# Long convolution and soft MoE: the convolution's first transform stage with tokens stationary, its results in one on-chip buffer, and the filter's spectrum read from DRAM

## The chip, the cores and the metric

The kernel runs on one core of one Trainium2 chip, in 32-bit floating point. The metric is the device time of one execution in microseconds; lower is better. Before the change three runs took 925.19, 927.99 and 931.83 us, median 927.99.

The engines go by short names: PE is TensorE's matmul and PEld its weight load, DVE is VectorE, ACT is ScalarE, POOL is GpSimd, SP is SyncE, which issues most DMAs here. A matmul of 32-bit numbers stands in the records twice (two passes, each with its weight load), so counts of records are twice the counts of matmuls.

## The reference

```python
def _attn_ref(x, h):                 # x (8, 5696, 128), h (5696, 128)
    L = 2 * S
    Xf = np.fft.rfft(x, n=L, axis=1)
    Hf = np.fft.rfft(h, n=L, axis=0)
    return np.fft.irfft(Xf * Hf[None], n=L, axis=1)[:, :S, :]

def _moe_ref(x, phi, w1, w2):        # x (45568, 128), phi (128, 32), 8 experts of 4 slots
    logits = x @ phi
    d = softmax of logits over the tokens
    slot_input = d.T @ x
    slot_out[e] = np.maximum(slot_input[e] @ w1[e], 0) @ w2[e]
    c = softmax of logits over the slots
    return c @ slot_out
```

A causal convolution of each of 128 channels with its own filter, along 5696 tokens and for 8 sequences ("batches"), and then a soft mixture of experts over all tokens.

## The kernel before, in words

The transform of length 2 x 5696 is split as N1 = 90 by N2 = 64: token 64 m + n is row m (89 rows, on partitions) and column n (64). A sequence passes through three stages. The filter h is treated as sequence 0, the batches as 1 to 8, so stages A and B run nine times, stage C eight times.

**Stage A** (`load_x` L179, `fold` L196, `stage_a` L205) works in eight steps per sequence. A step loads 4 columns and their 4 mirror columns (`xc`, three buffers, two DMAs), folds them into a sum and a difference on POOL (L201, 128x512), and multiplies each by two of the three tables in `s1`, which are stationary (L212: 128x128 weights, 512 moving columns: 4 columns by 128 channels). ACT copies each PSUM bank to `fst` (L214), and SP writes it to the DRAM buffer `f` (L218, two DMAs per half step, 1 KB runs).

**Stage B** works on frequencies. `f` is read back frequency by frequency into `gt` (`load_g` L230, 512 KB, up to two units ahead). A unit is two pairs of frequencies, 12 units per sequence. `stage_b1` (L241) does 8 matmuls of 64x64 weights by 256 columns (L250) into the PSUM tile `bt`; DVE multiplies `bt` by the real and the imaginary part of the filter's spectrum (L270, `Hr`, `Hi`, both kept on chip), and the products are added and subtracted into `yf` (L279: one of the two on POOL while `share` holds, that is before stage C begins and after stage A has ended, else both on DVE). For sequence 0 the same code makes `Hr` and `Hi` (L274). `stage_b2` (L283) does 8 more matmuls (L294) into `bz`, ACT copies them to `zst` (L299) and SP writes them to the DRAM buffer `z` (L302). `bt` and `bz` have one buffer each.

**Stage C** takes 8 columns ("a pair" T, 32 in all): `zc` is read from `z` (`load_pair` L322, one buffer), `stage_c1` (L336) finishes the inverse transform with matmuls (L349), a fold on DVE (L354, L355) and four adds on POOL (L368); `stage_c2` transposes (L377, ACT L379), `stage_c3` multiplies by phi (L386, ACT L389), `column_max` (L393) keeps a running maximum on DVE, `stage_c4` and `softmax` make both softmaxes (L411, L444), `dispatch` (L455) adds into the slots' sums, `stage_c6` stores the token weights. One pair takes two steps.

**The order of the work is written out by hand** in the loop at L563, and each engine does its instructions in that order. Step t does stage A of chunk t, stage B nine steps behind (LAG_B), stage C from step 27 on (LAG_C). Within a step: first half of stage A, `dispatch`, slot 1 of stage B, `stage_c1`, `stage_c2`, `stage_c6`, slot 2, `load_pair`, `load_x`, `stage_c5`, second half of stage A, `stage_c3`, slot 3, `column_max`, `softmax`. Steps have one unit of B (slot 2) and two units (slots 1 and 3) in turn. `stage_b2` of a unit comes in the slot after its `stage_b1`. Stage A ends after step 71, stage B after step 80. Then come the last pairs, the experts (L739 to L794) and the output (L809 to L836).

The four PSUM banks that `bank()` hands out in turn serve stages A and C together.

## Time and profile before

| what | value |
|---|---|
| median of three runs | 927.99 us |
| the profiled execution | 923.88 us, its span 922.1 us |
| mean granted TensorE clock | 0.943 |
| PE, DVE, ACT, POOL busy | 818.0, 653.1, 481.7, 488.1 us |
| stage A on PE (L212) | 576 records, 275.9 us |
| folds on POOL (L201) | 144, 192.8 us, 1342 ns each |
| stage A's evictions on ACT (L214) | 288, 171.9 us, 597 ns each |
| first matmul of stage B (L250) | at 52.65 us |
| DMA: f<-fst, gt<-f, z<-zst | 288 x 180 KB, 99 x 512 KB, 88 x 512 KB |
| the DMA queue of SP | 270.85 MB, 91.4% of the 16 engines' span |

How to read the profile: times are microseconds from the span's start unless marked ns. A group of instructions is line, engine, operation, output<-inputs, shapes and count, then busy time and the mean ns of one, then the idle time of its engine before them with what ended it. PE's matmuls are pipelined and the ends of their records are modelled, so a PE that is busy need not be at its peak, and the spacing of starts says more than a duration. A DMA engine counts as busy while it has a packet. Idle time of an engine that nobody waits for costs nothing.

### The profile page before, as it was taken

What the parts mean: (1) busy time and instruction counts of PE and PEld (TensorE: products, weight loads), DVE (VectorE), ACT (ScalarE), POOL (GpSimd) and SP (SyncE); (2) the same over time, 40 slices, a digit from 0 to 9 for tenths busy, and PEclk for the clock granted to TensorE, in tenths of its full rate; (3) what the DMA queues carried; (4) which work ended last, traced back from release to release, by engine and by line L of the source; (5) the groups of instructions that cost most, each with busy time, mean ns of one, the idle gap of its engine ahead of it and who ended that gap; (6) DMA issues with size and microseconds to landing.
All of it is one profiled execution on the core that took longest, in us unless ns stands there. A gap on an engine that the chain in (4) does not pass through costs nothing.

```text
span 922.1 us, 19325 instructions
## 1 busy us (share of the span) xinstructions
PE 818.0 (89%) x7220; PEld 423.9 (46%) x7220; DVE 653.1 (71%) x887; ACT 481.7 (52%) x888; POOL 488.1 (53%) x426
## 2 busy tenths in 40 slices
PE   6968898899999999999999999999987777878893
PEld 2323344345444445544554454444444434345783
DVE  3047665478888878888888788988887775674552
ACT  4623454455556655555666666656553344475442
POOL 4648766546655565556565655655466552472000
PEclk9989999899999999999999999999999888798865
DMA  9989999999899999999999999999989887761798
GB/s 298 279 274 299 272 345 311 289 345 327 268 320 319 314 282 324 316 314 285 341 304 327 289 324 329 297 318 320 316 269 330 272 254 198 211 249 73 272 405 341
DMA packets 156552, 272.45 MB, mean 295 GB/s; under 512 B 11766, under 2 KB 114422, under 8 KB 153317
## 3 DMA queue, kind: packets, MB, share of 16 engines
q1 hardware_dynamic: 155883, 270.85, 91.4%
q8 instruction: 58, 0.95, 0.4%
q10 hardware_dynamic: 576, 0.36, 0.2%
q14 instruction: 35, 0.29, 0.1%
HBM read 142.86 MB, written 128.21 MB: 294 GB/s over the span
## 4 chain that ended last, share of the span: by engine, by line
PE 51%; DMA 31%; POOL 5%; DVE 5%; issue 3%; SPq 2%; ACT 2%; DVEq 0%; POOLq 0%; ACTq 0%
PE bank L212 17%; DMA zc<-z 11%; PE bank L349 9%; DMA gt<-f 8%; PE bt L250 7%; PE bz L294 6%; DMA out_dram<-o 4%; PE bank L377 4%; DVE p L270 2%; POOL y L368 2%; DMA f<-fst 2%; PE bank L462 2%; DMA z<-zst 2%; PE bank L438 2%; PE bank L386 2%
## 5 line engine op out<-in xcount | busy, mean ns | idle before, releaser
L212 PE MATMUL bank<-x,s 128*128 128x512 f32 x576 | 275.9, 614 | 12.3 <-POOL x L201 12.0
L201 POOL TENSOR_TENSOR x<-xc 128x512 f32<-128x512 f32 x144 | 192.8, 1342 | 154.7 <-PE bank L212 70.4
L214 ACT ACTIVATE fst<-bank 128x512 f32<-128x512 f32 x288 | 171.9, 597 | 95.5 <-PE bank L212 74.8
L299 ACT ACTIVATE zst<-bz 128x1024 f32<-128x1024 f32 x96 | 93.2, 971 | 205.4 <-PE bz L294 198.5
L270 DVE TENSOR_TENSOR p<-bt,Hr 128x1024 f32<-128x1024 f32 x96 | 112.9, 1176 | 108.0 <-PE bt L250 95.7
L212 PEld LDWEIGHTS bank<-x,s 128*128 128x128 f32 x576 | 102.4, 193 | 131.5 <-issue 93.4
L279 DVE TENSOR_TENSOR yf<-p 128x512 f32<-128x512 f32 (+1 forms) x163 | 146.4, 931 | 3.3
L250 PE MATMUL bt<-gt,wt 64*64 64x256 f32 x1620 | 116.4, 394 | 25.1 <-DMA gt<-f 22.0
L349 PE MATMUL bank<-zc,i 128*64 128x512 f32 x480 | 117.1, 610 | 7.0 <-DMA zc<-z 4.1
L294 PE MATMUL bz<-yf,vt 64*64 64x256 f32 x1440 | 104.9, 393 | 15.5 <-POOL yf L279 15.0
L270 DVE TENSOR_TENSOR p<-bt,Hi 128x1024 f32<-128x1024 f32 x96 | 112.3, 1170 | 0.0
L250 PEld LDWEIGHTS bt<-gt,wt 64*64 64x64 f32 x1620 | 55.0, 134 | 102.0 <-issue 31.6
L368 POOL TENSOR_TENSOR y<-y,op 128x512 f32<-128x512 f32 x64 | 77.5, 1211 | 7.8 <-DVE op L354 5.1
L294 PEld LDWEIGHTS bz<-yf,vt 64*64 64x64 f32 x1440 | 58.2, 137 | 44.2 <-POOL yf L279 21.0
L279 POOL TENSOR_TENSOR yf<-p 128x512 f32<-128x512 f32 (+1 forms) x29 | 45.9, 1583 | 53.9 <-DVE p L270 53.9
L368 POOL TENSOR_TENSOR y<-y,om 128x512 f32<-128x512 f32 x54 | 71.8, 1330 | 2.1
L270 DVE TENSOR_TENSOR p<-bt,turn 128x1024 f32<-128x1024 f32 (+1 forms) x24 | 27.2, 1174 | 57.8 <-PE bt L250 57.7
L349 PEld LDWEIGHTS bank<-zc,i 128*64 128x64 f32 x480 | 30.8, 138 | 68.3 <-issue 40.8
L377 PE MATMUL bank<-ident,y 109*128 109x109 f32 x512 | 60.0, 275 | 0.7 <-DVE y L368 0.7
L377 PEld LDWEIGHTS bank<-ident,y 109*128 109x128 f32 x512 | 53.5, 151 | 13.6 <-issue 11.9
L379 ACT ACTIVATE yt<-bank 128x360 f32<-128x360 f32 x128 | 50.9, 482 | 3.3 <-PE bank L377 3.3
L819 PE MATMUL op<-so,cT 32*128 32x128 f32 x704 | 46.0, 374 | 4.4 <-ACT o L828 3.6
(97 smaller groups left out, 851.5 us busy)
## 6 DMA issues: line engine op xcount, KB each, us to landing
f<-fst SPq DMA_DIRECT2D x288, 180.0 KB
gt<-f SPq DMA_DIRECT2D x99, 512.0 KB
z<-zst SPq DMA_DIRECT2D x88, 512.0 KB
zc<-z SPq DMA_DIRECT2D x30, 1024.0 KB
xc<-in_x_dram SPq DMA_DIRECT2D x64, 320.0 KB
out_dram<-o SPq DMA_DIRECT2D x16, 1024.0 KB
zc<-z SPq DMA_DIRECT2D x30, 416.0 KB
out_dram<-o SPq DMA_DIRECT2D x8, 768.0 KB
```

The source lines that it names most:

```text
L201: nc.gpsimd.tensor_tensor(out=y_[:, :, :], in0=t_[:, 0, :, :], in1=t_[:, 1, ::-1, :], op=AL.subtract if comp else AL.add)
L212: nc.tensor.matmul(p[:, :], s1[:, tab[G], :], src[:, :, :].rearrange("p n d -> p (n d)"), start=True, stop=True)
L214: nc.scalar.activation(st[:, :, G, :], p[:, :].rearrange("p (n d) -> p n d", d=D), AF.Copy)
L250: nc.tensor.matmul(bt[q * HP:(q + 1) * HP, a, o, :], wt[r, 2 * i + q, :], t_[r, 2 * o + q, :, :].rearrange("p c d -> p (c d)"), start=True ...
L270: nc.vector.tensor_tensor(out=p_[r, 0:k, :, :], in0=pv, in1=h_, op=AL.mult)
L279: eng.tensor_tensor(out=y_[r, 0:k, c, :], in0=pr[r, 0:k, c, :], in1=pi[r, 0:k, 1 - c, :], op=op_)
L294: nc.tensor.matmul(bz[a * HP:(a + 1) * HP, q, o, :], vt[r, i, a, :], y_[r, a * m + o, :, :].rearrange("p c d -> p (c d)"), start=True, sto ...
L299: nc.scalar.activation(st[:, 0:m, 0:n, :].rearrange("p o q x -> p q o x"), bz[:, 0:n, 0:m, :], AF.Copy)
L349: nc.tensor.matmul(p[h_ * HP:(h_ + 1) * HP, :], i1[0:kr, tab, :], t_[0:kr, h_, o, :, q, :], start=True, stop=True)
L368: eng.tensor_tensor(out=part_, in0=part(v, 0), in1=o_[:, :, :], op=sign)
L377: nc.tensor.transpose(p[:, i * TR:(i + 1) * TR], ys[T][0:TR, k * CH + i, 0:D], ident[0:TR, 0:TR])
L379: nc.scalar.activation(yt[:, k * CH:(k + 1) * CH, :, :], of_tokens(p), AF.Copy)
```

## The change

- **Stage A with the tokens stationary.** The folded tokens become the weights (32 columns at a time, one channel, all 128 partitions) and the tables the moving operand (90 columns; 96 in every fourth matmul). One matmul gives 32 tokens by 90 table columns; four of them (sum and difference, two halves of the table) go to the four 32-column tiles of PE and fill the 128 partitions of one bank, four channels to a bank. A step of stage A is now 16 channels with all tokens of the sequence, where it was 8 columns with all channels. So all of a sequence's folds come before its first matmul.
- **`xf`, one buffer for a whole sequence.** Folded tokens lie there in one of two layouts by the parity of the sequence; the fold of the next sequence's chunk writes the places that stage A's step has just read. The weights are read at a step of 512 bytes (even) or 16 bytes (odd sequences). The 16 difference folds of sequences 0 and 1 go to DVE.
- **`ft` in place of the DRAM buffer `f`.** An 8 by 8 array of blocks, read along one axis by stage B and written along it by stage A of the next sequence, axes exchanged from sequence to sequence. ACT writes it from PSUM (DVE half of it for sequence 0), reading PSUM at a step of 90.
- **Stage B's units.** Eight groups of six frequencies per sequence, one per step: unit 0 has two pairs, unit 1 one pair (the last group one pair and a single frequency): 16 units per sequence instead of 12, the same matmuls. Both units are done before the step's stage A; slot 3 is gone.
- **The filter's spectrum in DRAM.** `Hr` and `Hi` are no longer on chip; sequence 0 makes `ht`, which is stored (786 KB per step), and read back in each step of the other sequences, two buffers.
- **Order.** LAG_B 8, LAG_C 26, the last step 79. `load_x` has two buffers, six during sequence 0 (four of them in `zc`). The products are added in place in `pr`. The loads of w1 begin one step earlier. Step t: `dispatch`, slot 1, `stage_c1`, `stage_c2`, `stage_c6`, slot 2, `load_pair`, `stage_c5`, all of stage A, the fold of chunk t+8, `load_x` of chunk t+10, `stage_c3`, `column_max`, `softmax`.

```diff
-    s1 = apool.tile([P, 3, P], F32, name="s1", tag="s1", bufs=1)
+    s1 = apool.tile([P, 2, 2, 2 * NP + 6], F32, name="s1", tag="s1", bufs=1)
+    xf = apool.tile([P, 2, HALF * D], F32, name="xf", tag="xf", bufs=1)
+    ft = fconst.tile([P, NJ, NJ, 2 * KG, DG], F32, name="ft")
...
-    xf = [apool.tile([P, CH, D], F32, name=f"x{i}", tag=f"x{i}", bufs=1) for i in range(2)]
-    xcs = [apool.tile([P, 2, CH, D], F32, name=f"xc{i}", tag=f"xc{i}", bufs=1) for i in range(3)]
-    for t_ in xcs:
-        nc.vector.memset(t_[:, :, :, :], 0.0)
+    zring = [ypool.tile([P, 2, 2, CH, 2, D], F32, name="zc")]
+    xcs = [apool.tile([P, 2, CH, D], F32, name=f"xc{i}", tag=f"xc{i}", bufs=1) for i in range(2)]
+    first = xcs + [zring[0][:, h_, o, :, :, :].rearrange("p n c d -> p (n c d)").rearrange(
+        "p (s n d) -> p s n d", s=2, n=CH)
+                   for h_ in range(2) for o in range(2)]
+    for i, t_ in enumerate(first):
+        (nc.gpsimd if i % 2 else nc.vector).memset(t_[:, :, :, :], 0.0)
...
-        t_ = xcs[c % len(xcs)]
+        t_ = first[c % len(first)] if g == 0 else xcs[c % len(xcs)]
...
-    folded = {}
-
-    def fold(c, comp):
-        if c not in xs:
+    def block(t_, g, r, k):
+
+        return t_[r, k, :] if g % 2 == 0 else t_[r, :, k]
+
+    def across(t_, g, r, k):
+
+        return t_[r, :, k] if g % 2 == 0 else t_[r, k, :]
+
+    def token_views(comp):
+
+        v = xf[:, comp, :]
+        return (v.rearrange("p (m d) -> p m d", d=D),
+                v.rearrange("p (e m f) -> p e m f", m=HALF, f=CH))
+
+    def fold(c):
+        if c >= (B + 1) * NJ:
             return
-        t_ = xs.pop(c) if comp else xs[c]
-        y_ = xf[comp]
-        nc.gpsimd.tensor_tensor(out=y_[:, :, :], in0=t_[:, 0, :, :], in1=t_[:, 1, ::-1, :],
-                                op=AL.subtract if comp else AL.add)
-        folded[(c, comp)] = y_
-
-    def stage_a(c, comp):
         g, j = divmod(c, NJ)
-        src = folded.pop((c, comp))
-        tab = (0, 1) if comp == 0 else (1, 2)
-        st = apool.tile([P, CH, 2, D], F32, name="fst", tag="fst", bufs=5)
-        for G in range(2):
+        t_ = xs.pop(c)
+        for comp in range(2):
+            eng = nc.vector if comp and g < 2 else nc.gpsimd
+            even, odd = token_views(comp)
+            if g % 2 == 0:
+                to, ab = even[:, CH * j:CH * (j + 1), :], (t_[:, 0, :, :], t_[:, 1, ::-1, :])
+            else:
+                to = odd[:, :, CH * j:CH * (j + 1), :].rearrange("p e n f -> p n e f")
+                ab = [v.rearrange("p n (e f) -> p n e f", f=CH)
+                      for v in (t_[:, 0, :, :], t_[:, 1, ::-1, :])]
+            eng.tensor_tensor(out=to, in0=ab[0], in1=ab[1], op=AL.subtract if comp else AL.add)
+
+    def stage_a(c):
+        g, s = divmod(c, NJ)
+        W = 2 * NP
+        for m in range(DG // CH):
             p = bank()
-            nc.tensor.matmul(p[:, :], s1[:, tab[G], :],
-                             src[:, :, :].rearrange("p n d -> p (n d)"), start=True, stop=True)
-            nc.scalar.activation(st[:, :, G, :],
-                                 p[:, :].rearrange("p (n d) -> p n d", d=D), AF.Copy)
-        n0 = comp * HALF + CH * j
-        for a, p in enumerate((F0, F1)):
-            nc.sync.dma_start(
-                out=fd[g][a, n0:n0 + CH, :, :, :].rearrange("n q c d -> q n (c d)"),
-                in_=st[p:p + NP, :, :, :].rearrange("k n c d -> k n (c d)"))
-
-
-    gs, prods = {}, {}
+            for k in range(CH):
+                w_ = W + (2 * KG * NJ - W if k == CH - 1 else 0)
+                for comp in range(2):
+                    even, odd = token_views(comp)
+                    d = s * DG + m * CH + k
+                    x_ = odd[:, d // CH, :, d % CH] if g % 2 else even[:, :, d]
+                    for a in range(2):
+                        r = (2 * a + comp) * HALF
+                        nc.tensor.matmul(p[r:r + HALF, k * W:k * W + w_], x_, s1[:, comp, a, 0:w_],
+                                         start=True, stop=True)
+            v = p[:, 0:1]
+            v = bass.AP(tensor=v.tensor, offset=v.offset,
+                        ap=[v.ap[0], [2 * KG, NJ], [1, 2 * KG], [W, CH]])
+            to = across(ft, g, slice(0, P), s)[:, :, :, m * CH:(m + 1) * CH]
+            if g == 0 and m % 2:
+                nc.vector.tensor_copy(out=to, in_=v)
+            else:
+                nc.scalar.activation(to, v, AF.Copy)
+
...
-        g, w = divmod(u, NW)
-        return g, w, [(i, min(2, NP - 2 * i)) for i in range(2 * w, min(2 * w + 2, NU))]
-
-    def load_g(u):
-        if u >= (B + 1) * NW:
-            return
-        g, w, us = parts(u)
-        n = sum(k for _, k in us)
-        t_ = bpool.tile([P, 4, 2, D], F32, name="gt", tag="gt", bufs=3)
-        nc.sync.dma_start(
-            out=t_[:, 0:n, :, :].rearrange("p q c d -> p (q c d)"),
-            in_=fd[g].rearrange("a r q c d -> (a r) (q c d)")[:, 8 * w * D:(8 * w + 2 * n) * D])
-        gs[u] = t_
+        c, part = divmod(u, 2)
+        g, j = divmod(c, NJ)
+        i0, i1_ = (KG // 2) * j, min((KG // 2) * (j + 1), NU)
+        us = list(range(i0, i1_ - 1)) if part == 0 else [i1_ - 1]
+        return g, j, part, [(i, min(2, NP - 2 * i)) for i in us]
+
+    def spectrum(c):
+        if c not in hs:
+            hs[c] = bpool.tile([P, 2, KG * D], F32, name="ht", tag="ht", bufs=2)
+            if c == NJ - 1:
+                nc.gpsimd.memset(hs[c][:, :, :], 0.0)
+        return hs[c]
+
+    def load_h(c):
+        if NJ <= c < (B + 1) * NJ:
+            nc.sync.dma_start(out=spectrum(c)[:, :, :], in_=hd[c % NJ])
+
+    def store_h(c):
+        nc.sync.dma_start(out=hd[c], in_=hs.pop(c)[:, :, :])
 
     def stage_b1(u, share):
-        g, w, us = parts(u)
-        t_ = gs.pop(u)
-        tag = "bz" if g == 0 and w % 2 else "bt"
-        bt = bps.tile([P, 2, 2, 2 * D], F32, name="bt", tag=tag)
+        g, j, part, us = parts(u)
+        bt = bps.tile([P, 2, 2, 2 * D], F32, name="bt", tag="bz" if g == 0 and part else "bt")
         for o, (i, n) in enumerate(us):
             for a in range(2):
                 r = slice(a * HP, (a + 1) * HP)
                 for q in range(n):
+                    f_ = 2 * ((2 * i + q) % KG)
                     nc.tensor.matmul(bt[q * HP:(q + 1) * HP, a, o, :], wt[r, 2 * i + q, :],
-                                     t_[r, 2 * o + q, :, :].rearrange("p c d -> p (c d)"),
+                                     block(ft, g, r, j)[:, :, f_:f_ + 2, :].rearrange(
+                                         "p s c d -> p c s d"),
                                      start=True, stop=True)
...
-        tags = ("yf", "yf") if g == 0 and w % 2 else ("pr", "pi")
-        pr, pi = [bpool.tile([P, 4, 2, D], F32, name="p", tag=x, bufs=2 if x == "yf" else 1)
-                  for x in tags]
-        for p_, H_ in ((pr, turn[:, 0]), (pi, turn[:, 1])) if g == 0 else ((pr, Hr), (pi, Hi)):
+        pr = bpool.tile([P, 4, 2, D], F32, name="p", tag="pr", bufs=2)
+        pi = bpool.tile([P, 4, 2, D], F32, name="p", tag="pi", bufs=1)
+        ht = spectrum(u // 2)
+        h0 = part * (KG - 2) * D
+        hv = [ht[r, v, h0:h0 + k * D].rearrange("p (k d) -> p k d", d=D) for v in range(2)]
...
         if g == 0:
-            for c, op_, H_, eng in ((0, AL.add, Hr, nc.vector), (1, AL.subtract, Hi, nc.gpsimd)):
-                h_ = H_[r, w, :, :, :].rearrange("p a o d -> p (a o) d") if m == 2 else H_[r, w, :, 0, :]
-                eng.tensor_tensor(out=h_, in0=pr[r, 0:k, c, :], in1=pi[r, 0:k, 1 - c, :], op=op_)
+            for c, op_, eng in ((0, AL.add, nc.vector), (1, AL.subtract, nc.gpsimd)):
+                eng.tensor_tensor(out=hv[c], in0=pr[r, 0:k, c, :], in1=pi[r, 0:k, 1 - c, :], op=op_)
             return
-        y_ = bpool.tile([P, 4, 2, D], F32, name="yf", tag="yf", bufs=2)
         for c, op_, eng in ((1, AL.add, nc.gpsimd if share else nc.vector),
                             (0, AL.subtract, nc.vector)):
-            eng.tensor_tensor(out=y_[r, 0:k, c, :], in0=pr[r, 0:k, c, :],
-                              in1=pi[r, 0:k, 1 - c, :], op=op_)
-        prods[u] = y_
+            eng.tensor_tensor(out=pr[r, 0:k, c, :], in0=pr[r, 0:k, c, :], in1=pi[r, 0:k, 1 - c, :],
+                              op=op_)
+        prods[u] = pr
...
-        st = bpool.tile([P, 2, 2, 2 * D], F32, name="zst", tag="zst", bufs=3)
+        st = bpool.tile([P, 2 - part, 2, 2 * D], F32, name="zst", tag=f"zst{part}", bufs=2)
...
-    LAG_B, LAG_C = NJ + 1, 3 * NJ + 3
-    PER = [1, 2] * (NJ // 2)
-    assert sum(PER) == NW
+    LAG_B, LAG_C = NJ, 3 * NJ + 2
     NA, NC = (B + 1) * NJ, B * NJ
-
-    def units(t):
-        g, i = divmod(t - LAG_B, NJ)
-        if t < LAG_B or g > B:
-            return []
-        return [g * NW + k for k in range(sum(PER[:i]), sum(PER[:i + 1]))]
-
-    steps = NC + LAG_C + 2
-    queue = [(u, t) for t in range(steps) for u in units(t)]
-    last_front = queue[-1][1]
-    AHEAD = 2
-    loaded = 0
-
-    load_x(0)
-    nc.scalar.dma_start(out=s1[:, :, :], in_=t_s1)
-    for c in range(1, 3):
+    last_front = NA + NJ - 1
+
+    for c in range(len(first)):
         load_x(c)
...
+    for c in range(NJ):
+        fold(c)
+        load_x(c + len(first)) if c + len(first) < NJ else None
+        if c >= NJ - 2:
+            load_x(c + 2)
...
     for t in range(last_front + 1):
-        us = list(units(t))
+        us = [2 * (t - LAG_B) + k for k in range(2)] if t >= LAG_B else []
+        share = t < LAG_C or t >= NA
...
-        turns = {2: (1, 3), 1: (2,)}.get(len(us), ())
-
-        def slot_b(place=None):
-            if place is not None and place not in turns:
-                return
+        def slot_b():
             fresh = bool(us)
             if fresh:
                 u = us.pop(0)
-                prefetch(u + AHEAD)
-                stage_b1(u, t < LAG_C or t >= NA)
+                stage_b1(u, share)
                 wait_b2.append(u)
+                if u % 2:
+                    c = u // 2
+                    if c < NJ:
+                        store_h(c)
+                    else:
+                        del hs[c]
+                    load_h(c + 1)
             if len(wait_b2) > fresh:
                 stage_b2(wait_b2.pop(0))
 
-        if t < NA:
-            stage_a(t, 0)
-            fold(t + 1, 0)
         if pair(3) is not None:
             dispatch(pair(3))
-        if t < last_front:
-            slot_b(1)
+        slot_b()
...
-        slot_b(2)
+        slot_b()
         if pair(-2) is not None:
             load_pair(pair(-2))
-        if t < NA:
-            load_x(t + 3)
-        if t == NJ:
-            prefetch(AHEAD)
         if U is not None:
             stage_c5(U)
         if t < NA:
-            stage_a(t, 1)
-            fold(t + 1, 1)
+            stage_a(t)
+            fold(t + NJ)
+            load_x(t + NJ + 2)
         if pair(1) is not None:
             stage_c3(pair(1))
-        slot_b(3)
         if pair(1) is not None:
             column_max(pair(1))
```

## The prediction

> **What bounds the kernel now.** I read the page's shares first, then the busy time by stage, then the timeline inside a stage, then the chain of waits.
>
> ```profile
> span 922.1 us, 19325 instructions
> ...
> PE 818.0 (89%) x7220; PEld 423.9 (46%) x7220; DVE 653.1 (71%) x887; ACT 481.7 (52%) x888; POOL 488.1 (53%) x426
> ...
> DMA  9989999999899999999999999999989887761798
> ```
>
> TensorE and the DMA engines are both near full for most of the span; that says only that the stages must be read apart. The busy time by stage (engine times, clock, DMA share, GB/s):
>
> ```profile
> core 0: us, PE busy (x) PEld busy (x) DVE busy (x) ACT busy (x) POOL busy (x), PEclk, DMA share, GB/s
> 101.00:180.70 79.70, 68.80 (x523) 30.96 (x521) 44.57 (x46) 36.29 (x54) 51.30 (x37) 0.96 0.96 311
> 180.70:661.40 480.70, 469.74 (x4149) 234.97 (x4145) 405.74 (x540) 286.06 (x520) 277.69 (x241) 1.00 0.99 313
> ...
> 672.70:756.50 83.80, 65.94 (x746) 35.95 (x744) 66.02 (x95) 36.22 (x67) 48.75 (x43) 0.94 0.88 286
> ```
>
> Line one is ten steps of stages A and B alone (8.0 us each), line two the 44 steps in which stage C runs too (21.9 us a pair of steps), line three the end, without stage A. In line two PE has 98% and DVE 84%. In line three stage A is gone and a pair still takes 20.8 us. So something other than stage A holds a pair near 21 us; the chain of waits there names it:
>
> ```profile
> 707.58 1.05 POOL L L431
> 708.63 1.15 POOL y L368
> ...
> 713.76 1.23 POOL yf L279
> ...
> 715.04 1.98 PE bz L294 x16
> ```
>
> It runs DVE folds, POOL, PE, ACT, the column maximum on DVE, and round again. Taking PE time out of stage A can win little more than that loop leaves.
>
> **The change, part by part.**
>
> *Stage A on PE.* Out: per step four matmuls of 512 columns, each twice (8 records). In: 16 channels x 4 matmuls x 2 = 128 records, 32 stationary columns, 90 moving (every fourth 96), in the four column tiles. The nearest row is a matmul of that form at the end:
>
> ```profile
> 497.02 3.60 PE L212 MATMUL bank<-x,s 128*128 128x512 f32 x8
> ...
> 851.95 3.70 PE L785 MATMUL bank<-w2s,hidT 128*32 128x128 f32 x128
> ```
>
> L212: (3.60 - 0.6 for the last one's own length) / 7 = 0.43 us per 512 columns, 0.84 ns a column. L785: (3.70 - 0.27) / 127 = 27 ns a record, 108 ns for four, which is 128 columns x 0.84: four tiles stream side by side and their 128 weight columns load under them. The trace's start times agree (851.954, 852.087, 852.197 for the first of each four), and the first weights show bare only 133 - 110 = 23 ns, so the four loads go side by side too. For 91.5 columns: 77 ns and 2 of overhead, 79 a group, x 32 = 2.5 us a step against 3.44. No row loads weights faster than 128 columns in 108 ns, and none loads strided ones, as the new tokens are (4 bytes every 512 or every 16). Bounds: 79 ns if hidden; 108 ns (3.45 us, no gain) if the loads hold it; for strided loads one after the other, ScalarE's price of a strided read:
>
> ```profile
> L379 ACT ACTIVATE yt<-bank 128x360 f32<-128x360 f32 x128 | 50.9, 482 | 3.3 <-PE bank L377 3.3
> ...
> L508 ACT COPY cT<-cl 128x352 f32<-128x352 f32 x12 | 10.0, 889 | 3.7 <-DMA cl<-c_t 3.7
> ...
> L491 ACT ACTIVATE cT<-bank 128x90 f32<-128x90 f32 x14 | 2.8, 263 | 6.1 <-PE bank L486 6.1
> ```
>
> L508 reads SBUF by single elements, (889 - 180) / 352 = 2.0 ns each, against 0.84 in L379; four loads of 32 would be 256 ns a group, 8.2 us a step. I take 79, since L785 is the only row of this form and a single load of 32 x 2.0 = 64 ns still fits under 79.
>
> Two rules of the Trainium skill speak against this. TensorE: Matmul & The Clock Gate, Part 3, says a weight load overlaps a running matmul only when their row groups differ; here all have all 128 rows. By that, 4 loads of 27 ns and 79 would be about 186 ns a group and 6 us a step, and the sum would end near 1,050 us (an estimate from that page). L785 has the same row groups and shows 108, so the rule does not hold there. SBUF — State Buffer, Specifications, says a read that crosses to a new 16-byte line each time pays a penalty; it gives no figure for TensorE, so it only says on which side to look; L508 is what this trace has.
>
> *Stage A's evictions.* Four of 512 elements (0.597 us, L214) become four of 384, read from PSUM at a stride of 90. L491 reads PSUM strided and writes short runs in 263 ns for 90, no dearer per element than L379. So 0.18 + 384 x 0.84 = 0.50 us; upper bound by L508, 0.95. ACT is at 60%; its cover is PE's 0.63 us a bank, and at 0.95 it would add some 1.3 us a step.
>
> *Folds.* Same 144, 16 of them to DVE. Odd sequences use runs of four elements: L201's 1.34 us at least, 1.84 x that (L508 against L379) = 2.5 at most. I take 1.34, since whole runs are nearer L201 than single elements. POOL has 42% idle, so this hides except where POOL is in the loop.
>
> *DMA.* f leaves: 288 writes of 180 KB in 1 KB packets, 51,840 x 49 ns / 16 engines = 159 us, and gt's reads, 165 us. In come 64 reads and 8 writes of 786 KB, at 293 ns per 5,760-byte packet 180 us. Engine time 843 to about 700 us, off the bound everywhere. Instruction records grow from 19,325 by 17,280; the instruction queue took 0.4% of the engines, so twice that is hidden.
>
> *Queues and new waits.* SP loses four f issues and one or two of gt a step and gains one of h. load_x now stands behind the fold that follows stage A (both folds end some 3 us into the next step), and the z store of unit 1 and the next h load stand behind load_x. The x it loads is wanted two steps later, and the h load (786 KB, 2.5 us at 313 GB/s and some 2 to land) by DVE's products of the next step, 5.8 us after it can start: hidden, at most 1 to 2 us a step on DVE if SP is held longer. xf and ft are single: a fold waits for stage A's matmuls (POOL then has nothing else due), and the first B unit of a sequence waits for stage A's last eviction, 0.3 to 0.8 us bare behind c3, 8 times, within the sum's rounding.
>
> *Stage B.* 12 units a sequence become 16, the same matmuls. DVE: 7 pairs and 9 single instead of 11 and 1: +0.3 us per two steps. The order is what costs. Stage A was interleaved with B; now both units come first and all of A last, so PE stands still until unit 0 is through DVE and POOL. Before, it looks like this:
>
> ```profile
> 123.41 1.09 PE L250 MATMUL bt<-gt,wt 64*64 64x256 f32 x16
> ...
> 124.63 1.22 DVE L270 TENSOR_TENSOR p<-bt,Hr 128x1024 f32<-128x1024 f32 x1 [2.81 <-PE bt L250]
> 125.77 1.21 DVE L270 TENSOR_TENSOR p<-bt,Hi 128x1024 f32<-128x1024 f32 x1
> ...
> 127.06 1.77 POOL L279 TENSOR_TENSOR yf<-p 128x512 f32<-128x512 f32 x1 [1.66 <-DVE p L270]
> ```
>
> Stage A's matmuls fill 125.3 to 127.2. After: b1 to DVE's start 1.22, two products and hand-over 2.43, POOL 1.83, b2 0.93, then stage A 2.5 = 8.9 us a step; the eighth, with one pair, 5.9.
>
> *Sum, by stage.* Start: all eight loads of h and 8 x 1.34 us of POOL folds now come before the first matmul, about 18 us (first load lands at 6.8) and 2 for the cold clock; 8 steps x 2.5 and an eviction: B starts at 41 instead of 52.7 (that wait was f's write and gt's read): -11.7. First eight B steps, POOL: 1.77 + 0.9 + 2.6 and gaps = 5.85 against 6.05: -1.6. Ten steps of line one: 9 x 8.9 + 5.9 = 86 against 79.7: +6.5. Pairs with stage C: PE streams 17.6 + 2.1 of changes = 19.7, but the loop is DVE's 18.9 less the 2.2 of unit 1, which falls beside PE, and then b2 0.9, stage A 2.5, c3 0.7, ACT 0.9 with gaps: 16.7 + 5.0 = 21.7 against 21.9; with one step more in this stage, +7. End: 8 steps at 9.4 (the same loop without stage A, 18.9 a pair) instead of 9 at 10.4: -18. Together -18: 923.9 (span 922.1 and 1.8 around it) becomes 906. The median of the runs is 4 us above the profiled one, so 910.
>
> **Rivals.**
> 1. *The weight loads hold PE.* At 108 ns a group +0.95 us in about 40 places that bind (8 at the start, 9 in line one, 23 pairs): +38, 948. The gain is gone from 18 / 40 / 32 = 14 ns more, 93 ns a group. At 256 ns PE binds each pair (19.7 + 2 x 5.7 = 31): +9.3 x 23, +51, +46 and about 25 in the first B steps: about 1,250. For it: strided weights appear in no row. Against it: L785's overlap.
> 2. *DVE and POOL get in each other's way.* Two L279 on DVE took 1.3 us beside an idle POOL and 3.25 at 498.5; odd folds at 2.5 us delay POOL's part in line one by 1.5 us x 8. One more microsecond per pair: +23 + 12: 945.
> 3. *PE's saving comes through.* If DVE's column maximum does not delay the next unit, pairs go at 19.7: -46 more, 866. DVE at 95% would be needed.
> 4. *The traffic is what bound.* DMA share 0.99 in line two. If PE waits were DMA's, 4 us less engine time a pair would show, as in 3; PE's idle there is 2%, which speaks against it.
>
> **How the numbers follow.** Forecast 0.38, with its own range 892 to 928; rival 1 at 108 ns 0.18, at 200 and more 0.12; rival 2 0.20; rivals 3 and 4 0.12. A measurement of this kernel tells about 1% from no change (919 to 937). Faster: 0.27 of the forecast's, and 0.12 = 0.39. Same: 0.11, 0.05 of rival 2, 0.03 of rival 1 = 0.19. Slower: the rest, 0.42. Range 870 to 980: it leaves out the dear end of rival 1 (0.12) and some of rival 3.
>
> **What would show it.** Right: stage A's records in fours 79 ns apart, 2.5 us a step; f gone and DMA share near 0.75; a first B matmul at 41 us; steps of 8.9 us without C, PE waiting there for POOL's p; pairs of 21.7 with DVE's multiply waiting on nothing and PE on DVE. Wrong: groups of 108 ns or more, ACT evictions over 0.6 us, odd folds over 1.6, a DVE wait for ht.

## The result and the profile after

The changed kernel takes 1081.72 us (median of four runs, 1074.5 to 1084.64) against 928.62 us of the kernel before on the same chip: 1.1638 times as long, interval [1.1567, 1.1709]. The forecast of 910 us and its range of 870 to 980 are both missed; the change costs 153 us. The profiled execution took 1074.5 us. Medians are of all runs of a kernel; the ratios leave out single runs that lie over 1.5% above the fastest of their kernel.

The page of the kernel after: span, busy time, the slices of the granted clock and of the DMA engines, and SP's queue and the instruction queue.

```profile
span 1072.4 us, 36094 instructions
...
PE 851.5 (79%) x15860; PEld 573.1 (53%) x15860; DVE 804.3 (75%) x1065; ACT 531.9 (50%) x904; POOL 526.1 (49%) x425
...
PEclk9999677889999999999999999999999898787855
DMA  7345455578666666777566577665445788856398
...
q1 hardware_dynamic: 95051, 221.29, 63.6%
q8 instruction: 125, 2.05, 0.8%
```

No engine is full any more. PE fell from 89% to 79%, the DMA engines from 91% to 64%, and still DVE is busy for 804 us where it was 653. Part of that is new work: e1_pitch33 below, in which every instruction of DVE is the same, has 705, so about 52 us are work and 99 us are instructions that take longer. An engine that takes longer for the same work is the first thing to look into. The busy time by stage (engine times, clock, DMA share, GB/s):

```profile
core 0: us, PE busy (x) PEld busy (x) DVE busy (x) ACT busy (x) POOL busy (x), PEclk, DMA share, GB/s
...
124.60:217.80 93.20, 68.33 (x1391) 49.35 (x1387) 41.42 (x48) 44.48 (x48) 43.08 (x32) 0.79 0.51 164
217.80:822.10 604.30, 515.88 (x10012) 339.85 (x10008) 517.70 (x661) 349.94 (x572) 306.05 (x240) 0.97 0.65 208
```

The first line is steps 16 to 23, without stage C; the second is steps 24 to 70, all but the first two of them with it. Where the time came from, counted by the starts of stage A's steps (step 0 is the first of the filter's eight):

| stretch | before | after | difference |
|---|---|---|---|
| to the start of step 8 | 39.8 | 64.1 | +24.3 |
| steps 8 to 16 (filter's stage B) | 54.9 | 60.5 | +5.6 |
| steps 16 to 26 (no stage C) | 77.7 | 114.0 | +36.3 |
| steps 26 to 71 (stage C too) | 489.0 | 583.6 | +94.6 |
| step 71 | 11.9 | 4.3 | -7.6 |
| stage A's end to stage B's | 86.8 | 83.3 | -3.5 |
| the rest | 162.0 | 162.7 | +0.7 |

The sum is 150.4, the difference of the spans. Most of it (130.9 us) lies in steps 16 to 71, where stage A runs beside stage B. The steps there are not alike: with stage C, a step of an odd sequence takes 11.4 to 11.8 us in the mean, one of an even sequence 14.0 to 14.4 us. The two differ in the layout of `xf` (and of `ft`, which the first experiment leaves alone): the weights' elements lie 512 bytes apart in even sequences, 16 bytes in odd ones. Two pieces of the timeline of the kernel after, columns: start, duration, engine, line, operation, tiles, shape, count, idle time before. First inside an even stage A:

```profile
559.81 4.56 PE L241 MATMUL bank<-s,xf 128*32 128x90 f32 x128
559.94 4.34 ACT L341 ACTIVATE zst<-bz 128x1024 f32<-128x1024 f32 x1 [3.66 <-PE bz L336]
560.91 3.28 DVE L321 TENSOR_TENSOR p<-p 128x256 f32<-128x256 f32 x2
...
573.03 2.52 DVE L394 TENSOR_TENSOR op<-bank,om 128x512 f32<-128x512 f32 x1
573.26 2.84 POOL L471 TENSOR_TENSOR L<-L,rm 128x512 f32<-128x512 f32 x1 [2.49 <-DVE rm L470]
```

and the same operations where an odd one begins:

```profile
468.76 1.03 ACT L341 ACTIVATE zst<-bz 128x1024 f32<-128x1024 f32 x1 [1.68 <-PE bz L336]
469.10 0.68 DVE L394 TENSOR_TENSOR op<-bank,om 128x512 f32<-128x512 f32 x1
469.21 2.26 PEld L241 LDWEIGHTS bank<-s,xf 128*32 128x32 f32 x112 [0.17 <-issue]
469.21 2.43 PE L241 MATMUL bank<-s,xf 128*32 128x90 f32 x111
469.32 1.05 POOL L471 TENSOR_TENSOR L<-L,rm 128x512 f32<-128x512 f32 x1 [2.61 <-DVE rm L470]
```

The reader is to see that one and the same eviction on ACT takes 1.03 us beside odd weight loads and 4.34 us beside even ones, DVE's fold 0.68 and 2.52, POOL's subtraction 1.05 and 2.84. It is no wait: the instructions themselves are long. Over the whole trace the mean for instructions of which at least 80% lies inside a step's stage A is, even against odd: zst 3063 and 1028 ns (28 and 11 of them), POOL's fold 3820 and 1294 (7 and 14), DVE's product of 512 elements 2471 and 681 (12 and 22). Not every instruction is hit: in the filter's eight steps, an even sequence, ACT's 16 evictions into `ft` keep 0.49 us, at 31.50 us for instance, while folds beside them on POOL (2.98 us) and DVE (3.05 us) are long; in the later even sequences the same evictions, where they run beside loads, take 1.08 us in the mean. Why, no run here shows. PE is hit as well: its groups of four records start 129 ns apart (median) in even sequences and 78 ns in odd ones, 4.9 and 2.8 us for a step's matmuls. In the kernel before ACT's copies are no longer beside stage A than elsewhere (512 elements 597 and 597 ns, 1024 elements 1024 and 1025); POOL's folds take 1368 and 1275.

Three lines of the waits of the kernel after (us in total, times, longest) show what else is there:

```profile
DVE mx L437 <- ACT lt L429: 79.3, 27, 6.7
...
PE bt L284 <- DVE p L309: 58.6, 35, 11.7
...
DVE p L309 <- DMA ht<-h_spec: 10.9, 5, 7.4
```

The first was 9.4 us before. The second's longest, and the third's, are one place, where the spectrum is first read back, between steps 15 and 16; lines of its timeline:

```profile
112.03 0.42 SPq L271 DMA_DIRECT2D ht<-h_spec  x1
...
118.40 2.36 DVE L309 TENSOR_TENSOR p<-bt,ht 128x1024 f32<-128x1024 f32 x2 [7.38 <-DMA ht<-h_spec]
...
120.91 1.13 PE L284 MATMUL bt<-ft,wt 64*64 64x256 f32 x8 [11.74 <-DVE p L309]
```

SP issues the load at 112.03, behind the last store of the spectrum; the data are used at 118.40, and PE stands for 11.7 us.

### The profile page after: what moved, and what is told of

Same layout as the page of the kernel before. It is cut to its first block, busy times and chain, and to the rows that moved or that the text cites. A ratio compares the mean times of both kernels' runs of the same rounds, so it can differ in the third digit from the quotient of the medians.

```text
span 1072.4 us, 36094 instructions
## 1 busy us (share of the span) xinstructions
PE 851.5 (79%) x15860; PEld 573.1 (53%) x15860; DVE 804.3 (75%) x1065; ACT 531.9 (50%) x904; POOL 526.1 (49%) x425
## 3 DMA queue, kind: packets, MB, share of 16 engines
q1 hardware_dynamic: 95051, 221.29, 63.6%
## 4 chain that ended last, share of the span: by engine, by line
DVE 34%; PE 28%; DMA 6%; ACT 5%; issue 4%; POOL 1%; DVEq 0%; SPq 0%; ACTq 0%; POOLq 0%
DVE p L309 13%; DVE p L321 10%; PE bank L389 6%; PE bz L336 6%; PE bank L241 5%; ACT zst L341 3%; DVE op L394 3%; DMA out_dram<-o 3%; PE bank L417 3%; PE bt L284 3%; DVE om L395 2%; DVE rm L470 2%; DMA zc<-z 2%; PE bank L426 2%; PE op L836 1%
## 5 line engine op out<-in xcount | busy, mean ns | idle before, releaser
L309 DVE TENSOR_TENSOR p<-bt,ht 128x512 f32<-128x512 f32 (+2 forms) x256 | 261.3, 1058 | 87.9 <-PE bt L284 72.5
L341 ACT ACTIVATE zst<-bz 128x512 f32<-128x512 f32 (+2 forms) x128 | 169.7, 1326 | 302.3 <-PE bz L336 288.4
L241 PE MATMUL bank<-s,xf 128*32 128x90 f32 (+1 forms) x9216 | 272.4, 278 | 39.0 <-POOL xf L226 20.5
L241 PEld LDWEIGHTS bank<-s,xf 128*32 128x32 f32 x9216 | 256.2, 190 | 68.6 <-issue 35.1
L226 POOL TENSOR_TENSOR xf<-xc 128x512 f32<-128x512 f32 x124 | 177.1, 1447 | 170.4 <-PE bank L241 165.7
L250 ACT ACTIVATE ft<-bank 128x384 f32<-128x384 f32 x272 | 149.7, 599 | 106.8 <-PE bank L241 99.7
L321 DVE TENSOR_TENSOR p<-p 128x512 f32<-128x512 f32 (+1 forms) x220 | 196.9, 933 | 4.4
L284 PE MATMUL bt<-ft,wt 64*64 64x256 f32 x1620 | 126.8, 401 | 65.9 <-DVE p L309 58.6
L336 PE MATMUL bz<-p,vt 64*64 64x256 f32 x1440 | 119.8, 428 | 69.8 <-DVE p L321 46.2
L336 PEld LDWEIGHTS bz<-p,vt 64*64 64x64 f32 x1440 | 54.0, 145 | 119.4 <-DVE p L321 64.3
L471 POOL TENSOR_TENSOR L<-L,rm 128x512 f32<-128x512 f32 x32 | 52.3, 1634 | 62.9 <-DVE rm L470 61.7
L417 PEld LDWEIGHTS bank<-ident,y 109*128 109x128 f32 x512 | 55.8, 155 | 13.0 <-issue 12.1
```

What stands on the lines that cost most here:

```text
L226: eng.tensor_tensor(out=to, in0=ab[0], in1=ab[1], op=AL.subtract if comp else AL.add)
L241: nc.tensor.matmul(p[r:r + HALF, k * W:k * W + w_], x_, s1[:, comp, a, 0:w_], start=True, stop=True)
L250: nc.scalar.activation(to, v, AF.Copy)
L284: nc.tensor.matmul(bt[q * HP:(q + 1) * HP, a, o, :], wt[r, 2 * i + q, :], block(ft, g, r, j)[:, :, f_:f_ + 2, :].rearrange("p s c d -> p c ...
L309: nc.vector.tensor_tensor(out=p_[r, 0:k, :, :], in0=pv, in1=h_, op=AL.mult)
L321: eng.tensor_tensor(out=pr[r, 0:k, c, :], in0=pr[r, 0:k, c, :], in1=pi[r, 0:k, 1 - c, :], op=op_)
```

## The experiments

Kernels of one group below ran on one chip with the kernel before, whose median was 929.2, 933.5, 931.8 and 926.3 us in the four groups. Ratios are to the kernel before, and are what is compared across groups.

### Group 1: the weights' step and the order

Theory S: the 512-byte step of the weights slows everything beside it. Rival O: the order (stage A's matmuls between b2 and c3) is what costs.

**e1_pitch33** and **e4_pitch34** pad `xf`, so that the weights of even sequences lie 528 or 544 bytes apart. In odd sequences the step stays 16 bytes, and the blocks of four channels move apart by the same padding; nothing else changes:

```diff
-    xf = apool.tile([P, 2, HALF * D], F32, name="xf", tag="xf", bufs=1)
+    PX = 33
+    xf = apool.tile([P, 2, HALF * PX * CH], F32, name="xf", tag="xf", bufs=1)
...
-        return (v.rearrange("p (m d) -> p m d", d=D),
-                v.rearrange("p (e m f) -> p e m f", m=HALF, f=CH))
+        return (v.rearrange("p (m d) -> p m d", d=PX * CH)[:, :, 0:D],
+                v.rearrange("p (e m f) -> p e m f", m=PX, f=CH)[:, :, 0:HALF, :])
```

> The rows of the folded tokens lie 528 bytes apart instead of 512 (one block of padding a row); nothing else. Theory S (weights read at a step of 512 bytes slow themselves and every other access to on-chip memory): even sequences become like odd ones, stage A 2.5 us a step instead of 4.0 to 4.5, ACT's zst of 1024 elements 1.02 us everywhere instead of 2.0, even steps 11.6 us instead of 14.4; start 15, sequence 2 20, sequences 4 and 6 22 each, sequence 8 18 us less: about 985 us (965 to 1005). Theory W (any strided weights, or something else of the even sequences): no change, 1065 to 1090. Theory O (the order of stage B and stage A alone): no change, 1065 to 1090.

> Rows 544 bytes apart, order as in the changed kernel. Theory S, in the form that only steps which fall on the same part of the memory again and again (512 bytes) conflict: the same as 528 bytes within 1%. If the step's size or its power of two counts in another way (544 is 2 x 272, 528 is 16 x 33): a different stage A time in even sequences, between 2.5 and 4.0 us.

Measured: 1011.14 us (1.0873 [1.0817, 1.0929]) and 1016.74 us (1.0951 [1.0913, 1.0989]). The same groups by form, of the kernel after and of e1_pitch33:

```profile
L341 ACT ACTIVATE zst<-bz 128x1024 f32<-128x1024 f32 x56 | 114.5, 2045 | 176.6 <-PE bz L336 167.3 <-DMA xc<-in_x_dram 7.5 <-DMA c_t<-cst 1.8
...
L471 POOL TENSOR_TENSOR L<-L,rm 128x512 f32<-128x512 f32 x32 | 52.3, 1634 | 62.9 <-DVE rm L470 61.7 <-PE bank L417 1.1
...
L394 DVE TENSOR_TENSOR op<-bank,om 128x512 f32<-128x512 f32 x32 | 42.0, 1312 | 3.9 <-PE bank L389 3.9
```

```profile
L342 ACT ACTIVATE zst<-bz 128x1024 f32<-128x1024 f32 x56 | 57.4, 1026 | 184.9 <-PE bz L337 158.0 <-DMA xc<-in_x_dram 20.8 <-DMA z<-zst 4.4
...
L472 POOL TENSOR_TENSOR L<-L,rm 128x512 f32<-128x512 f32 x32 | 33.6, 1050 | 61.6 <-DVE rm L471 61.5
...
L395 DVE TENSOR_TENSOR op<-bank,om 128x512 f32<-128x512 f32 x32 | 21.8, 682 | 4.7 <-PE bank L390 4.7
```

Sixteen bytes of padding bring ACT from 2045 to 1026 ns, POOL from 1634 to 1050, DVE from 1312 to 682: the means of the kernel before to about 1% (1024, 1048, 689). PE's groups of four in even sequences go from 129 to 79 ns. With 544 bytes it is the same (zst 1025 ns inside stage A). S holds, and it is worth 71 us. It is not all.

**e2_order** keeps the 512 bytes and turns the order; **e3_both** has both.

```diff
-        slot_b()
+        slot_b(hold=True)              # b1 of unit 1 alone
...
-        if t < NA:
-            stage_a(t)
-            fold(t + NJ)
-            load_x(t + NJ + 2)
         if pair(1) is not None:
             stage_c3(pair(1))
+        if t < NA:
+            stage_a(t)
+        if len(wait_b2) > 1:
+            stage_b2(wait_b2.pop(0))   # b2 of unit 0
+        if t < NA:
+            fold(t + NJ)
+            load_x(t + NJ + 2)
```

> The step of 512 bytes stays; only the order in a step changes: the second matmuls of unit 0 come after stage A instead of before it, and stage C's phi product before stage A. Theory O: PE's wait for DVE and POOL goes under stage A and the column maximum no longer waits behind it; the whole loss against before (150 us) goes, about 930 to 985 us. Theory S: odd steps fall from 11.6 to about 10.5 us (some 28 steps, -30 us), even ones by little since stage A still slows what now runs beside it: 1030 to 1075 us.

> Both edits together, 528 bytes and the new order. Theory S with the order as the second cause: all pairs of steps with stage C at about 20.5 to 21 us (PE streams 17.6 plus 2.1), so below the kernel before or level with it: 905 to 945 us. If S holds and the order costs nothing: same as the run with 528 bytes alone, about 985. Theory O alone: same as the run with the order alone.

Measured: e2_order 1043.79 us (1.1234 [1.1183, 1.1285]), e3_both 985.72 us (1.0602 [1.0544, 1.0661]). Both causes are real: 38 us by order alone, 25 more after the padding. DVE's wait for c3 (`mx` for `lt`) is 108.0 us in e1_pitch33 and 8.1 us in e3_both. But e3_both should have come to 905 to 945 us and is 57 us above the kernel before, so a third cause was missing. (In both orders stage A stays behind the second b1, because it overwrites the part of `ft` that b1 reads.)

### Group 2: two guesses for the 57 us

In e3_both DVE waits 32.6 us for `ht`, which is theory H: the read-back. And PE stops within runs of like matmuls for which nothing is missing ("issue"). If all records of PE are numbered (loads, matmuls, semaphore waits), 29 of 124 places that lie 256 records apart have a stop of over 0.2 us, 42.6 us in all. Theory F: PE runs out of instructions. The instruction queue brings them in packets of 16,384 bytes, 125 of them; for 32,000 records that is 256 to a packet. At none of the other 255 positions in such a block is there a single stop of over 0.2 us that waits for no semaphore. In the changed kernel itself these stops are 9, 7.6 us in all, and in e1_pitch33 12, 15.8 us: they grow as the other costs go.

**e5_early_h** asks for the next block at the start of a step, ahead of the z stores on SP. **e6_few** has a quarter of stage A's instructions, by 128 stationary columns. **e7_early_split** cuts stage A's run in two, **e8_early_few** puts e5 and e6 together.

```diff
# e5_early_h
-                    load_h(c + 1)            # after unit 1
...
+        if us:                               # first thing in the step
+            spectrum(t - LAG_B)
+            load_h(t - LAG_B + 1)
# e6_few: per bank 4 matmuls of 128 columns, 16 bytes apart
+                x_ = xf[:, comp, :].rearrange("p (n f) -> p n f", f=CH)[:, n:n + P, k]
+                nc.tensor.matmul(p[:, k * W:k * W + w_], x_, s1[:, comp, a, 0:w_],
+                                 start=True, stop=True)
# e7_early_split
         slot_b(hold=True)
+        if t < NA:
+            stage_a(t, range(2))
...
-            stage_a(t)
+            stage_a(t, range(2, DG // CH))
```

> The kernel with the 528-byte step and the new order (985.7 us), and one thing more: the next block of the spectrum is asked for at the start of a step, ahead of the step's z stores on SP, where it was asked for after unit 1. In the kernel it starts from, DVE waits 32.6 us for ht, 14 times, 4.2 to 7.0 us each in the first steps of sequence 1 (the load is issued behind a z store, and lands 6.0 to 6.4 us later). Theory H (the read-back is what is left): those waits go and lie on the path, 952 to 965, steps of sequence 1 without stage C at 8.9 or less instead of 9.75. Theory F (PE is short of instructions: in the trace PE stands still at 29 of 124 borders of 256 instructions, 42.6 us in all): this leaves those alone, so a wait that goes is partly replaced; 975 to 990. Theory N (16 units in one bt buffer and DVE's order): 978 to 990.

> The kernel with the 528-byte step and the new order (985.7 us), with stage A as 16 matmuls of 128 stationary columns in place of 64 of 32: the same moving columns, banks and evictions, a quarter of the instructions. It leaves out the right choice of tokens: stage A's numbers are meaningless, only its time is read. Theory F: the stops at the borders of 256 instructions (42.6 us) nearly go: 940 to 950 if the loads of 128 columns hide under 76 ns of streaming; if they show (108 ns a record, 3.5 us a step), 950 to 970. Theories H and N: nothing comes of fewer instructions, 980 to 990, and 990 to 1010 if the loads show.

> The kernel with the early read-back, and stage A in two halves with c5's and c3's matmuls between them, where it was one run of 128. Theory F: the instruction queue of PE gets a pause of 1 to 2 us between the halves in the steps with stage C, so some stops at the borders go: 8 to 20 us less than the kernel with the early read-back alone. Theories H and N: within 5 us of it.

> The early read-back and the stage A of 16 matmuls together (stage A's numbers meaningless again). If H and F both hold and are on the path: the sum of the two gains, 905 to 935, so at or below the time before the change (929). If only one holds: as that one alone. If N: 970 to 990.

Measured: e5_early_h 984.37 us (1.0553 [1.0497, 1.0609]): the waits for `ht` fall to 18.0 us and the time does not follow, so H alone falls. e7_early_split 983.85 us (1.0461 [1.0361, 1.056]): the two intervals overlap, and the stops are 50.2 us where e5_early_h has 44.2; a pause inside the step did not lessen them. e6_few 1313.35 us (1.4063 [1.4011, 1.4116]) and e8_early_few 1304.33 us (1.397 [1.3916, 1.4024]): far off, by something none of the theories had. Two groups of e6_few:

```profile
L240 PE MATMUL bank<-s,xf 128*128 128x90 f32 (+1 forms) x2304 | 558.1, 422 | 19.2 <-POOL xf L228 10.7 <-DMA zc<-in_h_dram 8.6
L240 PEld LDWEIGHTS bank<-s,xf 128*128 128x128 f32 x2304 | 543.1, 329 | 45.5 <-POOL xf L228 21.7 <-issue 17.4 <-PE bt L283 6.4
```

A step's 32 loads took 7.54 us, 236 ns for 128 columns that lie 16 bytes apart, 1.8 ns a column. That is the price at which L508 read single elements in the kernel before (2.0 ns), and the dear end of rival 1. Four loads of 32 such columns into the four column tiles take 78 ns together, so they do run side by side, and that alone made the change's stage A cheap. For F the run says nothing: its stops are gone, but its stage A is bound by the loads.

### Group 3: the instruction supply by itself

**e9_half** takes 64 stationary columns that lie side by side (an estimate of 54 ns at 0.84 ns a column), in two column tiles: the same streaming, half of the instructions, and no strided loads. **e10_early_half** adds e5's edit. **e11_before_many** goes the other way: the kernel before, its stage A cut into 16 times as many matmuls.

```diff
# e9_half
+                n = ((s * CH + m) * CH + k) * HALF
+                for a in range(2):
+                    r = 2 * a * HALF
+                    nc.tensor.matmul(p[r:r + 2 * HALF, k * W:k * W + w_], xf[:, a, n:n + 2 * HALF],
+                                     s1[:, a, 0, 0:w_], start=True, stop=True)
# e11_before_many, in the kernel before
-            nc.tensor.matmul(p[:, :], s1[:, tab[G], :],
-                             src[:, :, :].rearrange("p n d -> p (n d)"), start=True, stop=True)
+            for n in range(CH):
+                for r in range(0, P, 32):
+                    nc.tensor.matmul(p[r:r + 32, n * D:(n + 1) * D], s1[:, tab[G], r:r + 32],
+                                     src[:, n, :], start=True, stop=True)
```

> The kernel with the 528-byte step and the new order (985.7 us), with stage A as 32 matmuls of 64 stationary columns that lie side by side, in two column tiles, in place of 64 of 32: the same moving columns, banks and evictions, and the same 2.5 us of streaming, since a load of 64 columns at 0.84 ns (54 ns) hides under 76 ns. Half of stage A's instructions. It leaves out the right choice of tokens: stage A's numbers are meaningless, only its time is read. Theory F (PE's instructions come in blocks of 256, and a block that is used up in less than some 5 us makes PE stand still; 42.6 us in the kernel it starts from): most of that goes, 940 to 955, the eight steps at the start at 2.6 to 3.2 us instead of 4.74. Theory N (what is left is the 16 units and their buffers): 980 to 990.

> The same with the spectrum's block asked for at the start of a step (stage A's numbers meaningless). Alone, the early read-back gave 984.4 against 985.7, though the DVE waits for ht fell from 32.6 to 18.0 us. If it gave nothing because PE's stops took the place of those waits, it gives 8 to 15 us here, beneath the kernel with half of the instructions; if the read-back is covered, within 4 us of it.

> The kernel before, with each matmul of its stage A cut into 16 (4 column tiles x 4 tokens of 128 columns): the same results, the same streaming time (32 groups x 108 ns = 3.46 us a step against 3.44), no change in data, buffers or order, but 128 records a step where there were 8, so the instruction count of the changed kernel. Theory F: PE's stops at the borders of 256 instructions appear (there are none before), 20 to 40 us of them, and the time is 945 to 970; the eight steps at the start take 5 us or more instead of 3.94. If the number of instructions is not what costs: 925 to 934.

Measured: e11_before_many 961.94 us, 1.0348 [1.0265, 1.0432]. Nothing differs from the kernel before but the cut into more and narrower matmuls, and it is 30 us slower. They stream as fast (groups of four start 109 ns apart, 3.49 us a step against 3.44, at most 4 us over 72 steps). PE's timeline of e11_before_many in the first steps, where it has nothing to do but stage A:

```profile
17.71 3.83 PE L214 MATMUL bank<-x,s 128*32 128x128 f32 x127 [1.38 <-issue]
22.48 3.83 PE L214 MATMUL bank<-x,s 128*32 128x128 f32 x127 [0.94 <-issue]
26.47 3.84 PE L214 MATMUL bank<-x,s 128*32 128x128 f32 x127 [0.16 <-issue]
31.13 3.84 PE L214 MATMUL bank<-x,s 128*32 128x128 f32 x127 [0.81 <-issue]
35.51 3.75 PE L214 MATMUL bank<-x,s 128*32 128x128 f32 x127 [0.54 <-issue]
```

A run of 127 matmuls with their 127 loads (two semaphore waits make it 256), then a stop that waits for nothing the profile shows, and again. A step of stage A is 128 matmuls, so it is not the steps that set the beat. There are 38 stops of over 0.2 us, 41.7 us in all. The same in e3_both, where five borders within the filter's stage A cost 0.7 to 2.9 us each:

```profile
29.94 2.75 PE L242 MATMUL bank<-s,xf 128*32 128x96 f32 x128 [2.54 <-issue]
35.59 6.94 PE L242 MATMUL bank<-s,xf 128*32 128x96 f32 x256 [2.89 <-issue]
```

In the trace a packet of the instruction queue starts 2.0 us after PE has passed the border before (median of e3_both; 0.3 to 4.2 us for eight in ten), takes 1.0 us, and PE goes on 1.4 us after its end. That is 4.4 us in the middle and 6.6 in bad cases. It is no sharp limit. In e3_both, of the blocks that PE used up in under 5 us, 22 of 43 were followed by a stop; of those of 5 to 9 us, 7 of 47; of the longer ones none of 34. In e11_before_many it was 14 of 34, 23 of 71 and 1 of 19. The kernel before has 58 such packets, one in 16 us on average, and no such stops.

The Trainium skill, Runtime: NRT & Kernel Launch, section Instruction fetch mechanics, says that instructions come in blocks of 16 KiB, 256 instructions, and that the cost of crossing from one block to the next is mostly hidden. The block is what the trace shows; "hidden" holds for the kernel before and not for e11_before_many, which is 30 us longer.

e9_half: 970.29 us (1.0427 [1.0363, 1.0491]), less gain than forecast. No such stop is left, but the 64 columns reach into parts that the folds have just written: PE waits 32.7 us for `xf`, and sequence 0 grew by 10 us. e10_early_half: 950.2 us (1.0194 [1.0122, 1.0266]), 20 us less than e9_half.

### Group 4: what is left with all four edits

**e12_half_clean** takes the 64 columns where this step's folds don't write (as in e9_half it leaves out the right choice of tokens), **e13_early_clean** adds the early read-back, **e14_oldorder_clean** is e13 in the order of the changed kernel.

```diff
-                n = ((s * CH + m) * CH + k) * HALF
+                i = m * CH + k
+                n = 4 * PX * CH * s + 29 * i if g % 2 else PX * CH * i + DG * s
```

> As the kernel with half of stage A's instructions, but the 64 columns are taken where the folds of this step do not write (stage A's numbers meaningless). PE's wait for the folds goes, the first B matmul comes at 43 to 46 us (57.2 with all instructions), sequence 0 at 46 to 48 us. If the instruction supply is worth its 42.6 us: 945 to 955, that is 30 to 40 under 985.7. If it is not on the path, no less than 968.

> The same, with the spectrum's block asked for at the start of a step. If read-back and instruction supply hide each other, this is again some 15 to 20 us less: 926 to 938, the time before the change to within 1%; a fifth cause would show as 945 or more. The forecast of 910 would need pairs with stage C at 21.7 us; the last runs had 22.2 to 22.4.

> The same as that, in the order of the changed kernel: b2 of unit 0 ahead of stage A, c3 behind it. If the order costs what it did beside the 512-byte step or the 528-byte step (25 to 38 us): 950 to 975. If PE, no longer short of instructions, finds other work: within 10 us of the new order.

Measured: e12_half_clean 950.96 us (1.0284 [1.0208, 1.036]), e13_early_clean 936.44 us (1.0105 [1.0035, 1.0175]), e14_oldorder_clean 1000.08 us (1.0819 [1.0752, 1.0886]). In e12 and e13 the filter's stage A doesn't wait for all of the folds (it starts at 8.7 us), so their first 50 us are not to be compared. With that said, the costs in the order in which they were taken away, as ratios times 928.6: 152 us in all, 81 left after the padding, 56 after the order, 26 after half of the instructions, 10 after the early read-back. Of the 30 us of the third, 8.8 lie before step 8 (49.9 us against 58.7 in e3_both), where the waiting for the folds went as well, and the loads are no longer strided; e11_before_many is the cleaner measure. The early read-back is worth 15 us here by the medians, 17 by the ratios (the intervals of e12 and e13 do not meet), 20 between e9_half and e10_early_half, and nothing measurable while PE is short of instructions. It takes away little of the waiting for `ht`, though. DVE's line in e12_half_clean and in e13_early_clean:

```profile
DVE p L309 <- DMA ht<-h_spec: 44.6, 23, 7.1
...
DVE p L309 <- DMA ht<-h_spec: 39.2, 18, 5.2
```

So the read-back is not cured, it waits more than in the changed kernel (10.9 us), and where the 15 us come from was not shown.

e14_oldorder_clean shows the order's price when nothing covers it: 64 us. A line of its timeline, with the wait in brackets:

```profile
490.40 1.05 DVE L437 TENSOR_REDUCE mx<-lt 64x1 f32<-64x360 f32 x2 [4.82 <-ACT lt L429]
```

The column maximum stands in DVE's queue ahead of the next unit's products and waits for c3, and c3 waits behind stage A: 110.2 us in 30 waits, against 8.8 us in e13_early_clean.

The last 10 us of e13_early_clean are not settled by a run of their own. By the first matmuls of stage B, sequence 1, into which the first read-back falls, takes 75.3 us against 62.1 (+13.2), and sequences 2 to 8 together 5.0 us more. DVE waits 12.4 us for `ht` within sequence 1, so the read-back is the likeliest cause of most of these 10 us; no run settles it.

## Why the prediction was wrong

What it had right. The change's stage A in odd sequences: groups of four 78 ns apart (forecast 79). Evictions of 491 ns where nothing disturbs them (0.50), folds of 1.29 us (1.34) there. DMA: 63.6% of 1072.4 is 682 us of engine time (about 700). The first steps of B after the filter's stage A: 5.8 to 6.1 us (5.85). Stage A's first matmul at 19.9 us (20).

**Stage A on PE, 79 ns a group, everywhere.** This failed for five of the nine sequences. The prediction had bounded strided loads from both sides for PE and had 108 ns as a middle case, 948 us; the 129 ns found, in the even sequences alone, would have given about 955 by that sum (an estimate: 1.6 us in 8 + 8 + 12 of its places), inside the range. What it had not asked is what such loads do to others: it took stage A's cost to lie on PE alone. The runs showed most instructions of ACT, DVE and POOL at a half to a quarter of their pace as long as loads with a step of 512 bytes go on, and at full pace with 528, 544 and 16. Rival 2 looked for a slowing of DVE and POOL, but by each other, and at 1 us a pair.

The Trainium skill, SBUF — State Buffer, section SBUF: two separate sides, says that within the engines only the port shared by DVE and POOL makes for contention, and that PE and ACT never wait on anyone. This case disagrees: ACT's copy of 1024 elements went from 1028 to 3063 ns beside PE's loads. By the page's rule the padding would have left it as it was.

**Pairs at 21.7 us.** The loop was the right one (products, b2, stage A, c3, ACT, column maximum on DVE), its sum was not: 25.9 us (583.6 / 45 x 2), and in e14_oldorder_clean, without the 512 bytes and the stops, still 23.9 (537.1 / 45 x 2). The sum had two terms, DVE's work of 18.9 a pair and its idle time behind stage A: 5.0 us for b2, stage A, c3 and ACT less 2.2 that fall beside unit 1, 2.8 a pair. In the changed kernel it is the first that failed: DVE is busy for 22.6 us a pair (507.5 in these 45 steps), since its instructions are long, and waits 2.9 for c3 (66.3 us). With the padding it is the second: in e14_oldorder_clean DVE is busy for 19.2 (431.0) and waits 97.1 us for c3 in 22 waits, 4.4 each, 4.82 in the line above. In that step b2 comes after a wait for DVE's adds and takes 1.84 us for 0.9, and stage A takes 3.61 us at a granted clock of 0.74 for 2.5 (3.18 in the mean of the 45 steps). Moving three calls in the step was worth 25 to 64 us, and the prediction had charged the order with 6.5 us, in the ten steps without stage C, and a pair with nothing.

**Ten steps at 8.9.** 11.4 us a step; 10.5 in e14_oldorder_clean and 9.2 in e13_early_clean. The chain was as forecast; stage A in it was too small. In e14_oldorder_clean it takes 3.64 us in the mean of these steps where 2.5 were forecast, and 4.45 at a granted clock of 0.60 in the step at 138.93 us. Over steps 16 to 23 of the changed kernel the granted clock was 0.79, and the 2.5 us had come from a row at full clock (1.00 at L785).

**B starts at 41.** 61.9. From stage A's first matmul to B's, the filter's eight steps took 5.3 us each where 2.5 were forecast, and 4.6 in e3_both, where the step of the weights is cured. Here PE has no other work and uses its instructions up fastest: the stops at the borders are 3.8 us in this stretch of the changed kernel and 8.7 in e3_both. The prediction had looked at the instruction queue and had called it hidden, because its share of the DMA engines doubles from 0.4% only (0.8% was measured). The share did not tell of these stops: the price is in the time from border to border.

**The read-back hidden, at most 1 to 2 us a step.** Half wrong. Its first use cost 7.4 us of waiting on DVE and 11.7 on PE; the rest was hidden, but by the other costs: DVE's waiting for `ht` grew from 10.9 us to 44.6 as they went, and the early read-back was then worth 15 us.

**The end, -18.** -3.5 in the kernel after and -12.1 in e13_early_clean (74.7 us against 86.8), 9.3 us a step as forecast. Its size in the kernel before was over-counted.

Rival 4 (traffic) finds no support: the DMA share fell from 0.99 to 0.78 in the steps with stage C of e13_early_clean, and pairs took 22.0 us there (495.0 / 45 x 2) where the kernel before took 21.7 (489.0 / 45 x 2). Rival 3 (PE's saving comes through, 19.7) is not seen either. DVE is busy for 20.1 of the 22.0 us (452.0 in 45 steps) and waits 0.8 for `ht`, so even without that wait a faster stage A had little to give; that the chain through DVE, POOL and c3 sets the rest, as the prediction said, fits these numbers but was not tried by itself.

## What to carry to other kernels

When an operand's access pattern changes, ask not only what its engine pays but what its reads do to the others, and look for instructions that became longer, not only for waits; a few bytes of padding are a cheap trial. Count instructions per microsecond on the engine that gets many small ones: blocks of 256 that were used up in under 5 us were followed by a stop about half of the time here, and the queue that brings them was busy for 0.8% only. In an order written by hand, an instruction of DVE that waits for a late matmul holds up all that stands behind it; and costs that hide one another must be taken away together to be seen. So the price of each cost here holds for the order in which they were taken away.

## What the runs showed of the hardware that was not expected

- PE's loads of 32 columns with a step of 512 bytes lengthen most instructions of ACT, DVE and POOL that run beside them, 2 to 4 times (ACT 1028 to 3063 ns, DVE 681 to 2471 ns, POOL 1294 to 3820 ns). A step of 16, 528 or 544 bytes does not. ACT's evictions into `ft` in the filter's steps were not lengthened (0.49 us). Why 512 does it was not tried further: no other step was run.
- A load of 128 columns with a step of 16 bytes takes 236 ns; four loads of 32 into four column tiles take 78 ns together.
- PE's instructions come in packets of 16,384 bytes, 256 instructions. After blocks used up in under 5 us PE stood in 22 of 43 cases (e3_both) and 14 of 34 (e11_before_many), for up to 3.4 and 4.3 us; after blocks of over 9 us in none of 34 and 1 of 19.
